# Attention and two mixture-of-experts layers: VectorE's operands in PSUM, routing in eleven steps, and the second matmul of the first layer's tiles as three fp32r products

## The chip, the cores and the metric

One Trainium2 chip, one of its cores. The metric is the device time of one execution in microseconds (us); the time of a kernel is the median of its runs. TensorE is named PE here, VectorE DVE, ScalarE ACT, GpSimd POOL and SyncE SP, as the profile does.

## The reference, cut to what matters

```python
# attention: B=2, H=8, S=768, D=64, 16 clusters
q_assign = argmax(q_n @ c_n.T); k_assign = argmax(k_n @ c_n.T)     # per head
scores = where(q_assign[:, None] == k_assign[None, :], scale * q @ k.T, -1e9)
attn = exp(scores - max(scores)); attn /= attn.sum(-1) + 1e-9
x = attn @ v                                                       # to [1536, 512]
# first MoE: N=1536, D=512, E=8 experts, F=1024
do = x @ w_skip > 0; e = argmax(x @ w_gate); g = softmax(x @ w_gate)[e]
x = x + where(do, g * (relu(x @ w1[e]) @ w2[e]), 0)
# second MoE: the same, no skip, at most 384 tokens of an expert, no residual
out = g2 * (relu(x @ w1b[e2]) @ w2b[e2])
```

All tensors are float32. Expert choices hang on an argmax, so float32 accuracy is wanted nearly everywhere: a product either runs in native fp32, or both factors are split into a high part of type fp32r and a rest, and three fp32r products (high·high, high·rest, rest·high) are added up.

## The kernel before, in words

The program has three stages in one launch: attention, the first MoE layer, the second one.

**Attention** works on 16 heads (two batches of eight) in pairs; a pair is a *group* g, 0 to 7. A head has six key chunks of 128, and a head's chunk is a *unit* u = 6·head + chunk, so a group has 12 units and there are 96. In a unit PE makes the scores of one key chunk against all 768 queries (`score_mm`, L293, four matmuls of 128x384), ACT takes the exponential (L301, tile P) and casts it to fp32r (L302, tile Ph), POOL makes the rest Pl = P − Ph (L304), and three units later PE adds the chunk to the outputs in six matmuls (`pv`, L319, L321, L323). Ahead of a head, `mpass` (L273) makes the scores once more with queries on the partitions, and DVE takes the row maximum of each (L274, tile m; the two halves of the queries' keys are joined by L277). `mrow` turns these maxima into a row (psR, L281), which DVE subtracts into BB (L282); the head's scores can't begin before that.

A group is prepared during the group before it. For g from 2 on: `prep_T` transposes queries and keys on PE into a PSUM tile psT (L147) and ACT copies it to SBUF (qkT, L149); `prep_H` casts it to fp32r on DVE (qkH, L157) and `prep_L` makes the rest there (qkL, L163); both read and write SBUF alone. `prep_as` multiplies with the centroids (psA, L190), `prep_oh` finds each token's cluster on DVE (L220 to L224, scratch tile `ad` in SBUF), `prep_mk` makes the mask rows from it (psM, L239), and `prep_V` casts the values (VA, L173, DVE) and takes their rest (VL, L174, POOL). Groups 0 and 1 have a preparation of their own. A finished group is divided by its row sums (`fin_den`, `fin_nat`: xn, L362) and its gate logits are added up (lgt, L371, and lg, L378 to L380).

**The order** of PE, ACT, POOL and SP is the written one: a table `at(u, function)` says in which unit each piece stands, and `hooks` does the same for pieces of the MoE layer. DVE's order is made by the framework's scheduler. An engine runs its instructions strictly in order. All PSUM scratch of attention comes from one pool `ps_w` of six banks (tag "w"), taken in turn; the outputs have two more banks.

**Routing of batch 0** happens while batch 1 is still in attention: `early1` to `early4`, at units 58, 60, 63 and 65, choose two experts A and B and their tokens with some 60 small DVE instructions, nearly all from SBUF to SBUF; gathers follow at unit 67 and the two experts' weights from unit 68 and 84.

**The first MoE** (`run`) has 11 tiles of 128 tokens, t = 0 to 10: the two of batch 0's experts, eight routed ones (t = 2 to 9) and one for the rest. A tile is 8 steps of the first matmul (`l1_steps`, L973, 32 matmuls of 128x128, weights as they are, native fp32), a ReLU on ACT, and 8 steps of the second matmul (`l2n_steps`, L1028, one native fp32 matmul of 128x512 for each 128 of the 1024 hidden values). Table `at(t, step)` places the rest in between: e0 to e3 find the second layer's gate for the finished tile (ro and rg, L1096, are two matmuls among them), and the weights of tile t+2 are loaded at steps 8 and 16 of tile t.

**The second MoE** splits its weights (`split`: ACT casts wh, L950, DVE subtracts wl, L951) and its hidden values (hl, L1311), and makes its second matmul in three fp32r products (`l2`, L1022 to L1024).

Of the kernel before, what the change touches and what calls it, by code (L numbers as in the profile page):

```python
# [9 lines left out]
F32 = mybir.dt.float32  # L10
# [12 lines left out]
def attention(ctx, tc, q, k, v, centroids, wcat, lgacc, xa, xb, idw, hooks, bind):  # L23
# [82 lines left out]
    st = {}  # L106
# [21 lines left out]
    def prep_T(g, i):  # L128
# [20 lines left out]
        nc.scalar.copy(s["T"][:, sl], ps)  # L149
# [53 lines left out]
    def prep_oh(g, parts=((0, 2),)):  # L203
# [3 lines left out]
        d = sm.tile([128, C, 2, 2, NC], F32, name="ad", bufs=1)  # L207
# [4 lines left out]
        for a, b in parts:  # L212
# [8 lines left out]
            nc.vector.tensor_tensor(out=f(d), in0=l, in1=m.to_broadcast(G), op=ALU.subtract)  # L221
            nc.vector.scalar_tensor_tensor(out=f(d), in0=f(d), scalar=0.0, in1=f(w), op0=ALU.is_ge, op1=ALU.mult)
            nc.vector.tensor_reduce(out=m, in_=f(d), axis=AX.X, op=ALU.max)
            nc.vector.tensor_tensor(out=f(o)[..., 0:NC], in0=f(d), in1=m.to_broadcast(G), op=ALU.is_equal)  # L224
# [42 lines left out]
    def mpass(h, qc):  # L267
# [70 lines left out]
    def fin_w(g):  # L338
        nc.vector.tensor_copy(idw[:, 128:], wcat[:, g % HP].rearrange("p h n -> p (h n)"))
# [12 lines left out]
    def fin_nat(g, i):  # L352
# [15 lines left out]
        if i == 0:  # L368
            s["lgt"] = sm.tile([128, C, 2, W], F32, name="lgt")
        t = s["lgt"]  # L370
        nc.vector.tensor_tensor(out=t[:, cs], in0=ps[:, :, 128:N].rearrange("p c (h n) -> p c h n", h=2),  # L371
                                in1=r.to_broadcast([128, n, 2, W]), op=ALU.mult)
        if i == 0:
            return
        for hh in range(2):
            acc = lgacc[:, b]
            if j == 0 and hh == 0:
                nc.vector.tensor_copy(acc, t[:, :, hh, :])  # L378
            else:
                nc.vector.tensor_tensor(out=acc, in0=acc, in1=t[:, :, hh, :], op=ALU.add)  # L380
        del st[g]
# [34 lines left out]
    for g in range(NP):  # L416
# [13 lines left out]
        else:  # L430
            w = (-10, -7, -7) if g == 1 else [u + x for x in (-23, -23, -21)]
            for i in range(3):
                at(w[i], prep_T, g, i)
            w = [(-6, -5, -3), (-6, -5, -4)] if g == 1 else [[u + x for x in (-17, -17, -14)], [u + x for x in (-21, -18, -16)]]
            for i in range(3):
                at(w[1][i], prep_H, g, i)
                at(w[0][i], prep_L, g, i)
# [29 lines left out]
class Moe:  # L467
# [242 lines left out]
    def early2(self):  # L710
        self.pre0 = self.prefix(self.oh0, self.T0, self.C)
        self.cnt0 = self.ps()[:, 0:self.E]
        self.nc.tensor.matmul(self.cnt0, self.ones, self.T0[:, 0], start=True, stop=True)

    def early3(self):
        V, sm, E, C = self.nc.vector, self.at, self.E, self.C
# [3 lines left out]
        V.scalar_tensor_tensor(out=key, in0=self.cnt0, scalar=16.0, in1=self.w8[:, 0, :], op0=ALU.mult, op1=ALU.add)  # L720
        esA = self.pick(key, ab[:, 0], "pA", sm)
        V.scalar_tensor_tensor(out=key, in0=ab[:, 0], scalar=-65536.0, in1=key, op0=ALU.mult, op1=ALU.add)
        esB = self.pick(key, ab[:, 1], "pB", sm)
        self.eA = self.expert(esA, "dA", sm)
        self.eB = self.expert(esB, "dB", sm)
        self.relabel(esA, esB, sm)
        self.rank(self.oh0, self.pre0, C, "a", sm, r0)
        t = sm.tile([128, 2, C, E], F32, name="abt")
        ia = sm.tile([128, 2, C], F32, name="inAB")
        kp = sm.tile([128, C], F32, name="kp0")  # L730
        for i in range(2):
            V.tensor_tensor(out=t[:, i], in0=self.oh0, in1=ab[:, i].unsqueeze(1).to_broadcast([128, C, E]), op=ALU.mult)
        V.tensor_reduce(out=ia, in_=t, axis=AX.X, op=ALU.add)
        for i in range(2):
            V.scalar_tensor_tensor(out=ia[:, i], in0=r0, scalar=128.0, in1=ia[:, i], op0=ALU.is_lt, op1=ALU.mult)
        V.tensor_tensor(out=kp, in0=ia[:, 0], in1=ia[:, 1], op=ALU.add)
        V.tensor_scalar(out=kp, in0=kp, scalar1=-1.0, scalar2=1.0, op0=ALU.mult, op1=ALU.add)
        V.tensor_tensor(out=kp, in0=kp, in1=self.sel[:, 0:C], op=ALU.mult)
        V.tensor_tensor(out=self.oh0, in0=self.bc(self.mx0, E), in1=self.order.unsqueeze(1).to_broadcast([128, C, E]), op=ALU.is_equal)
        V.tensor_tensor(out=self.ohp[1][:, 0:C], in0=self.oh0, in1=self.bc(kp, E), op=ALU.mult)  # L740
        self.R0 = self.at.tile([128, C, 128], BF16, name="R0")
        self.make_R(self.R0, r0, 0, C)
        self.rhs0 = self.at.tile([128, C, 2, 2], BF16, name="rhs0")
# [488 lines left out]
    def run(self, lg, cap):  # L1232
# [111 lines left out]
        for t in range(n1):  # L1344
# [14 lines left out]
            if t:  # L1359
# [5 lines left out]
                if t > 1:  # L1365
                    at(t, 16, loads(t + 2, 4, 8))
# [176 lines left out]
```

## Time and profile before

| | us |
|---|---|
| runs (three) | 708.2, 708.95, 710.4; median 708.95 |
| profiled execution, its own time | 708.59 |
| its span in the trace | 706.6 |
| PE busy | 655.8 (93%) |
| DVE busy | 416.7 (59%) |
| ACT busy | 344.9 (49%) |
| POOL busy | 267.2 (38%) |

The profile is one execution. "Busy" is the time in which an engine had an instruction under way; PE's clock is listed apart, as the share of full speed that was granted. A releaser ("<-DVE m") is the instruction that ended a wait. Stages lie in the trace roughly so: attention from 5 to 320, first MoE to 484, second MoE to the end.

### The profile page before, as it was taken

To read this page: it belongs to the slowest core of one execution; us is meant where nothing else is said; L and a number is where in the kernel's file an instruction comes from. 1 tells how busy PE (TensorE), PEld (TensorE's weight loads), DVE (VectorE), ACT (ScalarE), POOL (GpSimd) and SP (SyncE) were. 2 spreads that over 40 slices of the span, in tenths; PEclk is the share of its full clock that TensorE was granted. 3 is DMA by queue.
4 is the path that set the end of the run, shared out by engine and by line. 5 is a ranking of instruction groups with operands and counts; after the bars stand their busy time and mean duration, and the time that the engine had idled before them with its cause. 6 is when DMAs were issued, how large, how long until landed. Compare 5 with 4: busy or idle time off the path is not lost. (4 is left out here: it accounts for less than half of the span.)

```text
span 706.6 us, 11607 instructions
## 1 busy us (share of the span) xinstructions
PE 655.8 (93%) x4174; PEld 550.9 (78%) x4174; DVE 416.7 (59%) x964; ACT 344.9 (49%) x580; POOL 267.2 (38%) x194
## 2 busy tenths in 40 slices
PE   7879999898988989999999999997899999999993
PEld 6858979797966868888777777776688899889983
DVE  6888787878799887515524322225556764656430
ACT  4757877686865668871111111113236464646330
POOL 6665767576765657830211111100313023202210
PEclk9889999999999999999999999999999999999997
DMA  7953837383834659042177778772295666476100
GB/s 222 220 108 83 201 77 192 71 198 67 202 68 90 192 126 319 29 133 61 56 262 264 288 292 308 297 284 77 58 393 211 238 253 215 146 263 246 34 31 4
DMA packets 78966, 121.55 MB, mean 172 GB/s; under 512 B 27569, under 2 KB 42929, under 8 KB 78896
## 3 DMA queue, kind: packets, MB, share of 16 engines
q1 hardware_dynamic: 74416, 108.18, 50.1%
q0 software_dynamic: 4480, 12.50, 5.4%
q8 instruction: 37, 0.61, 0.4%
q14 instruction: 33, 0.27, 0.1%
HBM read 87.90 MB, written 13.37 MB: 143 GB/s over the span
## 5 line engine op out<-in xcount | busy, mean ns | idle before, releaser
L304 POOL TENSOR_TENSOR Pl<-P,Ph 128x768 fp32r<-128x768 f32 x93 | 173.2, 1868 | 88.2 <-ACT Ph L302 60.1
L274 DVE TENSOR_REDUCE m<-psx 128x1 f32<-128x384 f32 x192 | 97.1, 548 | 30.2 <-PE psx L273 29.6
L301 ACT ACTIVATE P<-pss 128x384 f32<-128x384 f32 x192 | 84.7, 490 | 58.5 <-PE pss L293 56.0
L293 PE MATMUL pss<-BB,AA 128*128 128x384 f32 (+1 forms) x384 | 91.2, 362 | 11.9 <-DVE m L274 11.9
L951 DVE TENSOR_TENSOR wl<-l,wh 128x1024 fp32r<-128x1024 f32 x60 | 70.3, 1221 | 30.5 <-ACT wh L950 30.5
L302 ACT CAST Ph<-P 128x768 fp32r<-128x768 f32 x96 | 80.1, 834 | 7.0 <-PE pso L321 4.1
L973 PE MATMUL psl<-xt,l 128*128 128x128 f32 x640 | 79.1, 280 | 3.7 <-PEq L1155 3.7
L973 PEld LDWEIGHTS psl<-xt,l 128*128 128x128 f32 x640 | 76.2, 195 | 8.2 <-issue 8.2
L293 PEld LDWEIGHTS pss<-BB,AA 128*128 128x128 f32 (+1 forms) x384 | 68.2, 197 | 18.2 <-DVE m L274 15.8
L1028 PE MATMUL psl<-l,hn 128*128 128x512 f32 x160 | 74.4, 602 | 0.0
L319 PE MATMUL pso<-Ph,VA 128*65 128x384 f32 x192 | 67.5, 351 | 0.4 <-ACT DN L336 0.4
L321 PE MATMUL pso<-Ph,VL 128*64 128x384 f32 x192 | 67.8, 353 | 0.0
L323 PE MATMUL pso<-Pl,VA 128*65 128x384 f32 x192 | 66.9, 348 | 0.1
L1053 POOL DMA_INDIRECT out_dram<-y,fsi x15 | 15.5, 1035 | 132.8 <-ACT y L1052 126.0
L1306 PE MATMUL psl<-xh,wh 128*128 128x256 f32 x224 | 62.9, 281 | 2.2 <-DVE hl L1311 2.2
L1307 PE MATMUL psl<-xl,wh 128*128 128x256 f32 x224 | 62.4, 279 | 0.7 <-DVE xl L1296 0.7
L1308 PE MATMUL psl<-xh,wl 128*128 128x256 f32 x224 | 62.3, 278 | 0.0
L950 ACT CAST wh<-l 128x1024 fp32r<-128x1024 f32 x60 | 59.0, 1046 | 0.5 <-DVE acco L1097 0.5
L273 PE MATMUL psx<-AA,BB 128*128 128x384 f32 x192 | 51.9, 365 | 7.0 <-DVE m L274 5.9
L1045 POOL DMA_INDIRECT xb<-x,fsi x8 | 8.1, 1014 | 111.7 <-DVE Rt L1060 111.7
L1022 PE MATMUL psl<-wh,hh 128*128 128x512 f32 x120 | 48.3, 403 | 0.0
L1028 PEld LDWEIGHTS psl<-l,hn 128*128 128x128 f32 x160 | 27.5, 191 | 25.7 <-issue 25.4
(384 smaller groups left out, 1187.0 us busy)
## 6 DMA issues: line engine op xcount, KB each, us to landing
l<-in_moe_w_dram SPq DMA_DIRECT2D x136, 512.0 KB, 6.1
AA<-qkH SPq DMA_DIRECT2D x14, 384.0 KB, 3.9
vn<-in_v_dram SPq DMA_DIRECT2D x8, 384.0 KB, 5.8
BB<-qkL SPq DMA_DIRECT2D x16, 192.0 KB, 3.1
xa<-xn SPq DMA_DIRECT2D x8, 384.0 KB, 3.1
xb<-xn SPq DMA_DIRECT2D x8, 384.0 KB, 4.2
AA<-qkL SPq DMA_DIRECT2D x31, 96.0 KB, 3.4
BB<-qkH SPq DMA_DIRECT2D x31, 96.0 KB, 3.0
```

The lines of the kernel that those rows point to most:

```text
L274: nc.vector.tensor_reduce(out=hs[h]["m2"][:, qc, f:f + 1], in_=ps, axis=AX.X, op=ALU.max)
L293: nc.tensor.matmul(ps, AA[0:K, t, kc * 128:(kc + 1) * 128], BB[0:K, t, sl], start=(t == 0), stop=(t == 1))
L301: nc.scalar.activation(out=P[:, f * HF:(f + 1) * HF], in_=ps, func=AF.Exp, scale=1.0 / 8.0)
L302: nc.scalar.copy(Ph, P)
L304: eng.tensor_tensor(out=Pl, in0=P, in1=Ph.bitcast(F32), op=ALU.subtract)
L319: nc.tensor.matmul(o[0:D + 1, :], va, Ph[:, sl], start=(kc == 0), stop=False)
L321: nc.tensor.matmul(o[0:D, :], vl, Ph[:, sl], start=False, stop=False)
L323: nc.tensor.matmul(o[0:D + 1, :], va, Pl[:, sl], start=False, stop=(kc == C - 1))
L951: nc.vector.tensor_tensor(out=l, in0=src, in1=h.bitcast(F32), op=ALU.subtract)
L973: nc.tensor.matmul(st[k][:, q, :], L1[c][:, f * 128:(f + 1) * 128], xt[:, c, :], start=(c == 0), stop=(c == 3))
L1028: self.nc.tensor.matmul(ps, h[:, f, 0:128], L2[f // 2][:, f % 2, :], start=(f == 0), stop=(f == 7))
L1306: nc.tensor.matmul(ps[:, q, :], wh[:, fs], xh[:, c, :], start=(c == 0), stop=False)
```

## The change

In attention, for groups from 2 on, `prep_T` now makes three tiles from the PSUM tile at once: ACT casts qkH from it (the cast stands where the copy stood), DVE copies qkT from it, and DVE makes qkL = psT − qkH with psT as an operand. `prep_H` and `prep_L` remain for group 1 alone, and `prep_T` stands two to three units later. ACT casts VA for every group. The tile `ad` is gone: `prep_oh` works in place in the PSUM tile psA. The maxima of the two halves are joined by a reduction with one input. The logits are scaled in place in PSUM. Routing of batch 0 is written anew as a generator `early` of eleven steps, at units 58 to 73, each with a PSUM bank for its scratch values, so that an instruction has at most one operand in SBUF; gathers and expert A's loads stand eight units later, expert B's where they were.

In the first MoE, tiles 2 to 9 make the second matmul with `l2`: three fp32r products in place of one native fp32 matmul. For that, the next tile's four chunks of w2 are split during tile t at steps 2, 5, 9 and 12 (of tile 1 at 8, 10, 12, 14), the ReLU writes a high part h1 (ACT) and a rest h1l (DVE), and w2 of tile t+3 is loaded at step 16 of tile t, where that of t+2 was.

```diff
 def prep_T(g, i):
-        nc.scalar.copy(s["T"][:, sl], ps)
+        nc.scalar.copy(s["H"][:, sl], ps)
+        nc.vector.tensor_copy(s["T"][:, sl], ps)
+        nc.vector.tensor_tensor(out=s["L"][:, sl], in0=ps, in1=s["H"].bitcast(F32)[:, sl], op=ALU.subtract)
 def prep_V(g):
-        if g < 2:
-            nc.scalar.copy(VA[:, :, :, 0:D], src)
-        else:
-            nc.vector.tensor_copy(VA[:, :, :, 0:D], src)
+        nc.scalar.copy(VA[:, :, :, 0:D], src)
 def prep_oh(g):
-            nc.vector.tensor_tensor(out=f(d), in0=l, in1=m.to_broadcast(G), op=ALU.subtract)
+            nc.vector.tensor_tensor(out=l, in0=l, in1=m.to_broadcast(G), op=ALU.subtract)
...
 def mpass(h, c):
-            m2 = hs[h]["m2"]
-            nc.vector.tensor_tensor(out=hs[h]["m"], in0=m2[:, :, 0], in1=m2[:, :, 1], op=ALU.max)
+            nc.vector.tensor_reduce(out=hs[h]["m"], in_=hs[h]["m2"], axis=AX.X, op=ALU.max)
 def fin_w(g):
-        nc.vector.tensor_copy(idw[:, 128:], wcat[:, g % HP].rearrange("p h n -> p (h n)"))
+        nc.scalar.copy(idw[:, 128:], wcat[:, g % HP].rearrange("p h n -> p (h n)"))
 def fin_nat(g, i):
-        nc.vector.tensor_tensor(out=t[:, cs], in0=ps[:, :, 128:N].rearrange("p c (h n) -> p c h n", h=2),
-                                in1=r.to_broadcast([128, n, 2, W]), op=ALU.mult)
+        t = ps[:, :, 128:N].rearrange("p c (h n) -> p c h n", h=2)
+        nc.vector.tensor_tensor(out=t, in0=t, in1=r.to_broadcast([128, n, 2, W]), op=ALU.mult)
...
-            w = (-10, -7, -7) if g == 1 else [u + x for x in (-23, -23, -21)]
+            w = (-10, -7, -7) if g == 1 else [u + x for x in (-21, -20, -18)]
```

```diff
-    def early1(self, lg):
+    def early(self, lg):
...
+        mxp, dp, val = scratch(C, C * E, C * E)
+        dp, val = by(dp, E), by(val, E)
+        V.tensor_reduce(out=mxp, in_=l0[:, :, 0:E], axis=AX.X, op=ALU.max)
+        V.tensor_tensor(out=dp, in0=l0[:, :, 0:E], in1=self.bc(mxp, E), op=ALU.subtract)
+        V.tensor_copy(d, dp)
+        V.scalar_tensor_tensor(out=val, in0=dp, scalar=0.0, in1=self.w8[:, 0:C, :], op0=ALU.is_ge, op1=ALU.mult)
...
+        yield
...
+    def l2_steps(self, hh, hl, W2):
...
+            self.l2(hh, hl, W2(), range(f, f + 1), st[0])
...
 def run(...):
-                if t > 1:
-                    at(t, 16, loads(t + 2, 4, 8))
+                if t < n1 - 1:
+                    for i, x in enumerate((8, 10, 12, 14) if t == 1 else (2, 5, 9, 12)):
+                        at(t, x, lambda t=t, i=i: split(t + 1, 4 + i))
+                    at(t, 16, loads(t + 3, 4, 8))
...
+            if 1 < t < n1:
+                steps = steps + self.l2_steps(*hh, lambda t=t: [SP[t, i] for i in range(4, 8)])
...
+        er = moe.early(lg)
+        for i in (0, 1, 2, 4, 6, 8, 9, 11, 12, 13, 15):
+            hooks.setdefault(u0 + i, []).append(lambda: next(er))
```

How instructions stand, at three places. DVE in attention, where group 3 is prepared while group 1 is finished, before:

```order
L362 TENSOR_TENSOR xn<-psN,rden 128x384
L371 TENSOR_TENSOR lgt<-psN,rden 128x102
L339 COPY idw<-wcat 128x34
...
L157 CAST qkH<-qkT 128x512 x2
L163 TENSOR_TENSOR qkL<-qkT,qkH 128x512
L274 TENSOR_REDUCE m_1119<-psx 128x1 x2
L163 TENSOR_TENSOR qkL<-qkT,qkH 128x512
L157 CAST qkH<-qkT 128x512
L274 TENSOR_REDUCE m_1119<-psx 128x1 x4
L163 TENSOR_TENSOR qkL<-qkT,qkH 128x512
L277 TENSOR_TENSOR m<-m_1119 128x6
```

and with the change:

```order
L359 TENSOR_TENSOR xn<-psN,rden 128x384
L366 TENSOR_TENSOR psN<-psN,rden 128x3x34
L370 COPY lg<-psN 128x51
L372 TENSOR_TENSOR lg<-psN,lg 128x51
L150 COPY qkT<-psT 128x512
L151 TENSOR_TENSOR qkL<-psT,qkH 128x512
L272 TENSOR_REDUCE m_1104<-psx 128x1 x2
L150 COPY qkT<-psT 128x512
L151 TENSOR_TENSOR qkL<-psT,qkH 128x512
L359 TENSOR_TENSOR xn<-psN,rden 128x384
...
L274 TENSOR_REDUCE m<-m_1104 128x6
```

The three pairs of cast and subtraction became three pairs of copy and subtraction, with PSUM among their operands, and the row maxima (m) stand around them as before. ACT over the same stretch, with the change:

```order
L332 COPY OT<-pso_1321 64x384
L333 COPY DN<-pso_1321 1x384
L172 CAST VA_173<-vn 128x12x64
L298 ACTIVATE P<-pss 128x384 x2
L299 CAST Ph<-P 128x768
L149 CAST qkH<-psT 128x512
L298 ACTIVATE P<-pss 128x384 x2
L299 CAST Ph<-P 128x768
L149 CAST qkH<-psT 128x512
L298 ACTIVATE P<-pss 128x384 x2
```

The cast VA stands behind the copies of a finished head (OT, DN), and each cast qkH behind a unit's exponentials. DVE in one routed tile of the first MoE, with the change (x, Rt and Mj finish the tile before; tg to g3T are the second layer's gate, on which rg rests):

```order
L1088 SCALAR_TENSOR_TENSOR x_5173<-psl_5097,fgs,xg 128x512
...
L981 TENSOR_TENSOR wl<-l_0_4983,wh 128x1024
L1054 SCALAR_TENSOR_TENSOR h1l<-psl_5180,h_5178 128x512
L981 TENSOR_TENSOR wl<-l_1_4985,wh 128x1024
...
L1128 TENSOR_TENSOR ro<-Mj,ohT 128x96
L1054 SCALAR_TENSOR_TENSOR h1l<-psl_5214,h_5178 128x512
L981 TENSOR_TENSOR wl<-l_2_4987,wh 128x1024
L1141 TENSOR_TENSOR acco<-acco,psq 128x96
...
L1135 TENSOR_TENSOR rg<-Mj,g3T 128x36
L981 TENSOR_TENSOR wl<-l_3_4989,wh 128x1024
```

The wl and h1l rows are new there; the others stood there before in the same order.

## Rows read from the trace of the kernel before

**Rows 1.** Page, the head: span and instructions.

```profile
span 706.6 us, 11607 instructions
```

**Rows 2.** Waits of PE from 20 to 286 us: total, times, longest.

```profile
PE pss L293 <- DVE m L274: 11.9, 8, 3.4
PE psx L273 <- DVE m L274: 5.9, 4, 4.6
PE psR L281 <- DVE m L277: 3.7, 2, 2.3
PE psM L239 <- DVE oh L224: 2.8, 6, 0.5
```

**Rows 3.** Windows: PE, PEld, DVE, ACT, POOL busy, PE clock, DMA share, GB/s.

```profile
20.00:34.00 14.00, 12.26 (x65) 11.41 (x64) 12.09 (x24) 9.31 (x17) 8.46 (x7) 0.76 1.01 224
34.00:286.00 252.00, 228.57 (x1385) 197.61 (x1384) 206.88 (x400) 179.64 (x327) 165.40 (x91) 0.95 0.58 143
```

**Rows 4.** Groups of DVE, 70 to 320 us: busy, mean ns, idle before.

```profile
L274 DVE TENSOR_REDUCE m<-psx 128x1 f32<-128x384 f32 x149 | 75.7, 549 | 26.4 <-PE psx L273 25.9
L163 DVE TENSOR_TENSOR qkL<-qkT,qkH 128x512 fp32r<-128x512 f32 x15 | 20.3, 1375 | 0.0
L157 DVE CAST qkH<-qkT 128x512 fp32r<-128x512 f32 x15 | 13.3, 912 | 0.0
L173 DVE CAST VA<-vn 128x768 fp32r<-128x768 f32 x6 | 11.5, 1909 | 0.0
L277 DVE TENSOR_TENSOR m<-m 128x6 f32<-128x6 f32 x13 | 5.8, 450 | 0.1
```

**Rows 5.** Single lines, whole run: shortest/median/longest ns, first and last start us.

```profile
L157 DVE CAST qkH<-qkT x21: 410/421/3889, 7.5 to 244.3; 128x512 fp32r<-128x512 f32 x21
L163 DVE TENSOR_TENSOR qkL<-qkT,qkH x21: 676/693/2340, 7.9 to 249.8; 128x512 fp32r<-128x512 f32 x21
L277 DVE TENSOR_TENSOR m<-m x16: 152/154/1756, 24.4 to 291.1; 128x6 f32<-128x6 f32 x16
L362 DVE TENSOR_TENSOR xn<-psN,rden x16: 556/558/559, 79.9 to 319.2; 128x384 f32<-128x384 f32 x16
L142 DVE COPY qkT<-psT x2: 683/684/685, 16.9 to 19.8; 64x512 f32<-64x512 f32 x2
L171 ACT CAST VA<-vn x2: 830/836/842, 17.4 to 24.5; 128x768 fp32r<-128x768 f32 x2
L654 DVE COPY einf<-psq x1: 153/153/153, 234.7 to 234.7; 128x4 f32<-128x4 f32 x1
```

**Rows 6.** Timeline of DVE, 31 to 52 us: start, us, instruction.

```profile
41.02 4.04 DVE L157 CAST qkH<-qkT 128x512 fp32r<-128x512 f32 x2
44.98 4.52 DVE L163 TENSOR_TENSOR qkL<-qkT,qkH 128x512 fp32r<-128x512 f32 x2
```

**Rows 7.** Timeline of PE, 45 to 70 us.

```profile
50.02 1.47 PE L273 MATMUL psx<-AA,BB 128*128 128x384 f32 x3 [4.62 <-DVE m L274]
```

**Rows 8.** Timeline of PE, 395 to 430 us, a tile's second matmul.

```profile
403.96 1.88 PE L1028 MATMUL psl<-l,hn 128*128 128x512 f32 x4
405.68 0.21 PE L1096 MATMUL psq<-ro,Rt 128*128 128x96 bf16 x1
```

**Rows 9.** Timeline of PE, 528.8 to 534.5 us, a second matmul in three products.

```profile
528.88 0.40 PE L1022 MATMUL psl<-wh,hh 128*128 128x512 f32 x1
534.40 0.27 PE L961 MATMUL psxT<-idw,xg 128*128 128x128 f32 x1
```

**Rows 10.** Window of one routed tile, columns as in rows 3.

```profile
404.00:420.00 16.00, 16.00 (x101) 11.95 (x100) 3.80 (x19) 2.46 (x5) 2.03 (x2) 1.00 0.77 287
```

**Rows 11.** Single lines of the second MoE, columns as in rows 5.

```profile
L951 DVE TENSOR_TENSOR wl<-l,wh x60: 1215/1220/1228, 490.6 to 687.0; 128x1024 fp32r<-128x1024 f32 x60
L950 ACT CAST wh<-l x60: 1034/1046/1066, 482.0 to 685.5; 128x1024 fp32r<-128x1024 f32 x60
L1311 DVE SCALAR_TENSOR_TENSOR hl<-psl,hh x28: 684/691/693, 521.3 to 672.2; 128x512 fp32r<-128x512 f32 x28
```

More of the change, by code (lines that the diff above doesn't have):

```diff
@@ L379, in fin_nat @@
             else:
-                nc.vector.tensor_tensor(out=acc, in0=acc, in1=t[:, :, hh, :], op=ALU.add)
-        del st[g]
+                nc.vector.tensor_tensor(out=acc, in0=t[:, :, hh, :], in1=acc, op=ALU.add)
+        if i:
+            del st[g]
     sched = {}
@@ L430, in attention @@
         else:
-            w = (-10, -7, -7) if g == 1 else [u + x for x in (-23, -23, -21)]
+            w = (-10, -7, -7) if g == 1 else [u + x for x in (-21, -20, -18)]
             for i in range(3):
                 at(w[i], prep_T, g, i)
[L434 to L437, printed above, removed]
+            if g == 1:
+                for i, (l, h) in enumerate(zip((-6, -5, -3), (-6, -5, -4))):
+                    at(h, prep_H, g, i)
+                    at(l, prep_L, g, i)
             w = (-5, -4, -3) if g == 1 else [u + x for x in (-19, -17, -16)]
@@ L710, in early2 @@
[L710 to L716, printed above, removed]
-        r0 = sm.tile([128, C], F32, name="r0")
-        key = sm.tile([128, E], F32, name="key")
-        ab = sm.tile([128, 2, E], F32, name="ab")
[L720 to L730, printed above, removed]
-        for i in range(2):
[L732 to L743, printed above, removed]
-        self.rhs05 = self.at.tile([128, C, 2, 5], BF16, name="rhs05")
-        for i in range(2):
-            V.tensor_tensor(out=self.rhs0[:, :, i], in0=self.cols2[:, 0:C], in1=self.bc(ia[:, i], 2), op=ALU.mult)
-            V.tensor_tensor(out=self.rhs05[:, :, i], in0=self.cols5[:, 0:C], in1=self.bc(ia[:, i], 5), op=ALU.mult)
@@ L761, in relabel @@
         V.tensor_copy(self.namei, x)
-    def early4(self):
-        p1 = self.spread(self.R0, self.rhs0, self.C)
-        p2 = self.spread(self.R0, self.rhs05, self.C)
-        inf, t, S = self.ids(p1, 2, self.rt, "e")
+        V.tensor_copy(xs, x)
+        yield
+        ia = sm.tile([128, 2, C], F32, name="inAB")
+        ta = sm.tile([128, 2, C, E], F32, name="abt")
+        ks = sm.tile([128, C], F32, name="kp0")
+        abp, iap, kp = scratch(2 * E, 2 * C, C)
+        abp, iap = by(abp, E), by(iap, C)
@@ new lines, in early @@
+        V.tensor_copy(abp, ab)
+        for i in range(2):
+            V.tensor_tensor(out=ta[:, i], in0=abp[:, i].unsqueeze(1).to_broadcast([128, C, E]), in1=oh0, op=ALU.mult)
+        V.tensor_reduce(out=iap, in_=ta, axis=AX.X, op=ALU.add)
+        for i in range(2):
+            V.scalar_tensor_tensor(out=iap[:, i], in0=r0, scalar=128.0, in1=iap[:, i], op0=ALU.is_lt, op1=ALU.mult)
+        V.tensor_reduce(out=kp, in_=iap.rearrange("p i c -> p c i"), axis=AX.X, op=ALU.add)
+        V.tensor_scalar(out=kp, in0=kp, scalar1=-1.0, scalar2=1.0, op0=ALU.mult, op1=ALU.add)
@@ new lines, in early @@
+        V.tensor_tensor(out=ks, in0=kp, in1=self.sel[:, 0:C], op=ALU.mult)
+        V.tensor_copy(ia, iap)
+        yield
+        rhs0 = sm.tile([128, C, 2, 2], BF16, name="rhs0")
+        rhs05 = sm.tile([128, C, 2, 5], BF16, name="rhs05")
+        mxp, o, iap = scratch(C, C * E, 2 * C)
+        o, iap = by(o, E), by(iap, C)
+        V.tensor_copy(mxp, mx)
+        V.tensor_copy(iap, ia)
+        V.tensor_tensor(out=o, in0=self.bc(mxp, E), in1=self.order.unsqueeze(1).to_broadcast([128, C, E]), op=ALU.is_equal)
@@ new lines, in early @@
+        V.tensor_tensor(out=self.ohp[1][:, 0:C], in0=o, in1=self.bc(ks, E), op=ALU.mult)
+        for i in range(2):
+            V.tensor_tensor(out=rhs0[:, :, i], in0=self.bc(iap[:, i], 2), in1=self.cols2[:, 0:C], op=ALU.mult)
+            V.tensor_tensor(out=rhs05[:, :, i], in0=self.bc(iap[:, i], 5), in1=self.cols5[:, 0:C], op=ALU.mult)
+        yield
+        R0 = sm.tile([128, C, 128], BF16, name="R0")
+        for i in (0, 3):
+            self.make_R(R0, r0, i, i + 3)
+            yield
@@ L767, in early4 @@
+        inf, t, S = self.ids(self.spread(R0, rhs0, C), 2, self.rt, "e")
+        self.rest(self.spread(R0, rhs05, C), 2, S, self.rt, "e")
         self.dests(inf, t, 2, S, self.rt, "e")
-        self.rest(p2, 2, S, self.rt, "e")
         self.S1 = S
+        yield
     def route1(self, lg):
@@ L977, in l1_steps, with step @@
         return [lambda f=f: step(f) for f in range(8)]
+    def l2_steps(self, hh, hl, W2):
+        st = {}
+        def step(f):
+            if f == 0:
+                st[0] = self.ps2()
+            self.l2(hh, hl, W2(), range(f, f + 1), st[0])
+            return st[0]
+        return [lambda f=f: step(f) for f in range(8)]
     def l2n_steps(self, h, L2):
@@ L1033, in new_h, with new_h1 @@
         return hh, hl
+    def new_h1(self):
+        return [self.big.tile([128, 8, 128], F32R, tag=x, name=x) for x in ("h1", "h1l")]
     def new_hn(self, n):
```

123 lines of the change are left out of this document (77 added, 46 removed).

## The prediction, written before the run

> **What bounds the kernel now.** I read the page first: the span [rows 1] and the busy shares (the table above). PE's high share would say "PE-bound", but it is an average, so I went stage by stage with three views: PE's waits, windows of busy time with the granted clock, and DVE's groups by line.
>
> In attention the waits of PE between 20 and 286 us come from one place [rows 2]: DVE's row maxima m and, more rarely, the tile oh. The four rows add up to 11.9 + 5.9 + 3.7 + 2.8 = 24.3 us. No row there names ACT, POOL or a DMA. The windows say the same from another side [rows 3]: PE is busy 12.26 of 14 us and 228.57 of 252 us, so it stands still for 1.74 + 23.43 = 25.2 us. They also show a second loss: the mean granted clock is 0.76 and 0.95 of full speed. Where a stretch W ran at clock c, at most (1 − c)·W can be got back: 3.4 and 12.6 us. A wait and the clock go together: the longest wait, 4.62 us, ends at 50.02 [rows 7], and the stretch around it is one of those below full clock. So attention has 25.2 + 16.0 = about 41 us in which PE was waiting or slowed, of which 36.0 lie after 34 us.
>
> Why is m late? Its reduction is not slow: 549 ns on the average of 149 [rows 4]. What stands before it in DVE's order is. The cast qkH takes 421 ns at the median but 912 on the average after 70 us; qkL 693 and 1375; the tiny joining of two halves, 154 and 450 [rows 4, 5]. Their longest are 3889, 2340 and 1756 ns. An instruction of six elements that takes 1.76 us once isn't computing, it is held up. The excess over the median is 15 × 0.491 = 7.4 us for qkH, 15 × 0.682 = 10.2 for qkL and 13 × 0.296 = 3.8 for the joining. These lines read and write SBUF only. xn, with an operand in PSUM and one in SBUF, took between 556 and 559 ns in all 16 cases, and the copies from PSUM 683 to 685 [rows 5]. One place shows it whole: at 41.02 us two qkH took 4.04 us and two qkL 4.52 [rows 6], where the medians give 0.84 and 1.39. PE's 4.62 us of waiting ends right after [rows 7].
>
> In the first MoE there is nothing to wait for: in a routed tile PE is busy 16.00 of 16 us at full clock, DVE 3.80 and ACT 2.46 [rows 10]. That stage is bound by PE's own work.
>
> **The change part by part.**
> *qkT, qkH, qkL.* ACT does one cast where it did one copy: no more work. DVE copies T at 0.684 us and subtracts at 0.691, the price of hl, which has the same operands in the same places and size [rows 5, 11]. For the 15 of each in rows 4, DVE spent 20.3 + 13.3 = 33.6 us and will spend 15 × 1.375 = 20.6. Both prices hardly vary in their rows.
> *VA.* DVE loses 11.5 us; ACT gets 6 × 0.836 = 5.0 [rows 4, 5]. ACT was busy 179.64 of 252 us [rows 3], so this lies beside PE's work.
> *The joining of m*: 5.8 us become 13 × 0.154 = 2.0.
> *oh, logits, idw, the routing's small instructions*: the same arithmetic, more copies, fewer held up. A single small instruction costs the same either way (a 4-element copy from PSUM took 153 ns, the shortest joining in SBUF 152 [rows 5]). I cost this part at nothing: its held-up instructions and the additional copies roughly cancel. Its cover is DVE's slack; without it some 25 copies of 0.16 us, 4 us, would show.
> So DVE sheds 13.0 + 11.5 + 3.8 = 28 us of its 207, above all where m waits in line.
> What of the 41 us comes back? Lower end: nothing, if another wait takes over at once. Upper end: all of it. The 5.1 us before 34 us belong to groups 0 and 1, whose preparation hardly changes; I leave them. Of the other 36.0 I take five sixths, **30 us**: it is nearest to the upper end since all the waiting in rows 2 hangs on one engine, and the sixth is left for first halves of chains that DVE still has to compute (oh before the mask, BB before the scores).
>
> *Second matmul of eight tiles.* Native: two hidden blocks from 403.96 to 405.68, so 0.86 us each [rows 8]. In three products: eight blocks from 528.88 to 534.40, so 0.69 each [rows 9]. Saved: 8 tiles × 8 × 0.17 = 10.9 us. Added per tile: on DVE four wl of 1.220 and two h1l of 0.691, 6.3 us, to 3.80 + 6.3 = 10.1 of 14.6 us; on ACT four casts of 1.046, to 6.6 [rows 10, 11]. Both lie beside PE, but DVE's order puts the gate (rg) behind three wl, and rg is due two thirds through the second matmul. I take off 0.9 for that: **10 us**. The w2 loads move a tile ahead on SP's queue, behind slots that the split has freed by then; at 287 GB/s and a DMA share of 0.77 [rows 10] a tile of 14.6 us would need 0.84, so they stay hidden.
>
> The sum is 708.59 − 30 − 10 = **668.6 us**, made against the profiled execution, which lies 0.4 us below the median of the runs shown.
>
> [...] A copy of a few elements from PSUM took 153 ns where one instruction of that size in SBUF took 152 [rows 5]: no surcharge. [...]
>
> **The rivals.**
> *B: PSUM banks run short.* A psT bank was free after ACT's copy; now it is held through a cast, a copy of 0.684 and a subtraction of 0.691, 1.4 us longer, 18 times; psA is held through three more passes, some 1.6 us, 6 times; each routing step holds one too. All from six banks in turn. Against: no row of rows 2 waits for a bank. For: the margin isn't shown. Between nothing and 18 × 1.4 + 6 × 1.6 = 35 us; a third of it, 12, leaves attention 18 us, and with its gates later the MoE 9: 708.6 − 27 = 681.6 us.
> *C: the MoE tiles gain little.* If the splits hold DVE so that rg or the ReLU's rest comes late by 0.9 us in each of eight tiles, 7 of the 10 us go: 708.6 − 30 − 3 = 675.6 us.
> *D: the hold-ups stay*, that is, the change doesn't do what it says. Then the MoE's 10 us are all: 698.6 us. Against it stand the rows of xn and of the copies from PSUM, which never vary while POOL works beside them [rows 5]. [...]
> *E: slower.* The subtraction now waits in DVE's order for ACT's cast, and all later m stand behind it. ACT works 179.64 / 84 = 2.1 us per unit (252 us hold 84 units of 3 us) [rows 3]. DVE's slack after the change is 252 − 207 + 28 = 73 us, so 18 waits of over 73 / 18 = 4.1 us each would make DVE the bound. With two units' work and VA ahead of the cast, 4.2 + 0.8 = 5.0 us, attention grows by 18 × 0.9 = 17 us: 708.6 + 17 − 10 = 715.4 us. Against: the cast stands right behind one unit's exponentials, so 2 to 3 us are likelier; it decides only past 4.1.
>
> **How the numbers follow.** A has 62 in 100, B 20, C 10, D 4, E 3; one is left for a mishap that I can't name. The likeliest gives 668.6. Its own range is 659 (36 and 11 back, plus a little of the clock before 34 us) to 678 (attention two thirds of 30). For 8 in 10 over all cases the upper end must take in B with some 6 us more of its 35 lost: 659 to 687. A measurement of this kernel can tell some 0.3%, 2 us, from no change. A, B, C and D all lie further below than that: faster 0.96; the same 0.01; slower 0.03, from E.
>
> **What would show it.** Right: the copies and subtractions of rows 4's two lines at a steady 0.68 to 0.69 us, no small instruction of 1.8 us in routing, PE's waits on m below 8 us between 20 us and the end of attention, the clock there at 0.98 or more; second matmuls at 0.69 us a block and tiles every 14.6 us. Wrong: PE waiting for ACT's cast or for a bank's last reader (B, E), m waiting behind qkL while qkL waits for ACT (E), waits at the rg matmul (C), or DVE rows that still vary (D). If attention's end moves by 30 us and the total doesn't, loads of the first MoE's weights were the next thing late.

## The result, and the profile after

The changed kernel took 680.12 us (median of four runs, 677.97 to 681.07), the kernel before on the same chip 708.86; the ratio is 0.9587 with a 95% interval of 0.956 to 0.9615. Faster, then, and inside the range of 659 to 687, but 11.5 us above the 668.6 that I gave. The profiled execution took 680.39 us, its span is 678.7. So the two traces compared here lie 28.2 us apart, where the forecast had summed up 40.

Three marks on PE cut the program into pieces: attention's last output matmul, the last native second matmul of the first MoE (tile 10), and the end. The rows are for single lines: shortest, median and longest duration in ns, then the first and the last start. Kernel before:

```profile
L293 PE MATMUL pss<-BB,AA x384: 331/340/686, 28.0 to 308.4; 128*128 128x384 f32 x192
L323 PE MATMUL pso<-Pl,VA x192: 331/337/562, 36.5 to 312.9; 128*65 128x384 f32 x192
L1028 PE MATMUL psl<-l,hn x160: 592/593/677, 337.7 to 497.6; 128*128 128x512 f32 x160
```

Changed kernel:

```profile
L290 PE MATMUL pss<-BB,AA x384: 331/338/522, 26.7 to 286.7; 128*128 128x384 f32 x192
L320 PE MATMUL pso<-Pl,VA x192: 331/338/387, 33.8 to 291.4; 128*65 128x384 f32 x192
L1069 PE MATMUL psl<-l,hn x32: 592/592/676, 316.2 to 468.4; 128*128 128x512 f32 x32
```

Attention ends 312.9 − 291.4 = 21.5 us earlier; the stretch from there to the last native second matmul shrank from 184.7 to 177.0, 7.7 us; the rest of the program took 209.0 and then 210.3, 1.3 us more. 21.5 + 7.7 − 1.3 = 27.9, the difference of the spans. The 1.3 us are PE's busy time, 192.6 and then 193.8 us for the same 1305 instructions, at a granted clock of 0.98 and then 0.97; PE's idle time there is 16.5 us in both traces. Why the clock was granted less is not shown. I call the time from the first score to the last output matmul "attention's length": 284.9 us before, 264.7 now.

The views that carried the prediction, of the changed kernel. PE's waits from 20 to 286 us (against [rows 2]):

```profile
PE pss L290 <- DVE lg L372: 3.6, 4, 1.2
PE pss L290 <- ACT P L298: 2.1, 3, 1.0
PE psx L271 <- DVE m L272: 1.4, 3, 0.5
PE pss L290 <- DVE key L744: 1.2, 1, 1.2
PE psR L278 <- DVE m L274: 1.0, 1, 1.0
PE pss L290 <- DVE ab L748: 0.9, 1, 0.9
PE psx L271 <- ACT P L298: 0.9, 2, 0.7
PE pso L316 <- ACT DN L333: 0.7, 3, 0.2
PE pss L290 <- DVE m L272: 0.6, 2, 0.5
```

Windows, columns as in [rows 3]:

```profile
20.00:34.00 14.00, 12.05 (x67) 10.64 (x66) 13.21 (x27) 10.43 (x18) 9.63 (x7) 0.88 0.98 222
34.00:286.00 252.00, 240.46 (x1507) 206.07 (x1506) 170.59 (x425) 202.60 (x373) 178.59 (x99) 1.00 0.61 152
```

DVE's lines that stand where those of [rows 5] stood:

```profile
L150 DVE COPY qkT<-psT x18: 679/683/693, 39.5 to 218.3; 128x512 f32<-128x512 f32 x18
L151 DVE TENSOR_TENSOR qkL<-psT,qkH x18: 680/681/684, 40.1 to 219.0; 128x512 fp32r<-128x512 f32 x18
L274 DVE TENSOR_REDUCE m<-m x16: 166/166/170, 24.5 to 269.4; 128x6 f32<-128x12 f32 x16
```

What to read there: the durations became constant, as forecast. The granted clock after 34 us rose from 0.95 to 1.00. And PE's idle time fell only from 25.2 us to 1.95 + 11.54 = 13.5. The waits of pss and psx for m fell from 11.9 + 5.9 us to 0.6 + 1.4, but the scores (pss) now wait for other instructions than before: lg and ab, which are DVE's last readers of psN and of a routing bank, key, and ACT's P. (key reads no bank last. It ends at 210.08 us, an lg on psN at 210.01, and PE goes on at 210.16, 0.15 us after that lg as in the case below; so this wait, too, is one for psN's bank.)

Those windows hold different amounts of work. Over attention's length, which holds the same 1561 PE instructions in both traces, the first two columns and PE's clock are comparable (kernel before, then changed kernel):

```profile
28.00:312.90 284.90, 260.61 (x1561) 224.56 (x1561) 222.63 (x429) 207.09 (x377) 186.62 (x102) 0.95 0.57 139
26.70:291.40 264.70, 251.97 (x1561) 215.27 (x1561) 180.17 (x442) 212.19 (x391) 185.12 (x103) 0.99 0.61 151
```

So of the 20.2 us by which the length shrank, 24.3 − 12.7 = 11.6 are PE's idle time and 8.6 its busy time, in which the higher clock has a part that these rows don't part from the rest. The other 1.3 of the 21.5 us lie before the first score.

One of these new waits at close range. DVE, then PE, of the changed kernel; start, us, instruction:

```profile
107.13 0.56 DVE L359 TENSOR_TENSOR xn<-psN,rden 128x384 f32<-128x384 f32 x1 [0.45 <-PE psN L357]
107.79 0.27 DVE L366 TENSOR_TENSOR psN<-psN,rden 128x102 f32<-128x102 f32 x1
108.09 0.46 DVE L372 TENSOR_TENSOR lg<-psN,lg 128x51 f32<-128x51 f32 x2
```

```profile
106.93 0.60 PE L290 MATMUL pss<-BB,AA 128*128 128x384 f32 x2
108.70 0.59 PE L290 MATMUL pss<-BB,AA 128*128 128x384 f32 x2 [1.17 <-DVE lg L372]
```

A score matmul reads BB and AA and writes a scratch bank; it has no business with lg except that lg is the last to read the bank. PE goes on 0.15 us after it.

The two longest of [rows 2] have to be read in the same way. A matmul of psx or pss doesn't read m either; the reduction m (L274) is the last reader of a psx bank. DVE, then PE, of the kernel before:

```profile
122.52 4.57 DVE L163 TENSOR_TENSOR qkL<-qkT,qkH 128x512 fp32r<-128x512 f32 x2
127.01 1.94 DVE L274 TENSOR_REDUCE m<-psx 128x1 f32<-128x384 f32 x4
```

```profile
122.64 0.89 PE L273 MATMUL psx<-AA,BB 128*128 128x384 f32 x4
123.55 0.30 PE L190 MATMUL psA<-cblk,qkT 128*128 128x32 f32 x2
...
125.10 0.52 PE L293 MATMUL pss<-BB,AA 128*128 128x384 f32 x2
127.61 2.29 PE L293 MATMUL pss<-BB,AA 128*128 128x384 f32 x6 [1.99 <-DVE m L274]
```

Four tiles psx, one psA and one pss (two matmuls each) take the six banks in turn; the next score wants the first psx's bank, and starts when the first of the four reductions, late behind two held-up qkL, has read it. So 11.9 + 5.9 = 17.8 of the 24.3 us of [rows 2] were waits for a bank: the kernel before was short of banks already whenever DVE was late.

In the first MoE, a tile's second matmul (PE's timeline, first two hidden blocks, and the next tile's first):

```profile
365.90 0.48 PE L1063 MATMUL psl<-wh,h 128*128 128x512 f32 x1
366.22 0.40 PE L1064 MATMUL psl<-wh,h1l 128*128 128x512 f32 x1
...
367.38 0.22 PE L1140 MATMUL psq<-ro,Rt 128*128 128x96 bf16 x1
367.42 0.48 PE L1063 MATMUL psl<-wh,h 128*128 128x512 f32 x1
...
380.77 0.48 PE L1063 MATMUL psl<-wh,h 128*128 128x512 f32 x1
```

The period is 380.77 − 365.90 = 14.87 us where it was 16.00. A product starts every 0.23 us, but the first one behind another kind of matmul takes 0.32.

### The profile page after: what moved, and what is told of

It is laid out like the page before. It is cut to its first block, busy times and chain, and to the rows that moved or that the text cites. A ratio compares the mean times of both kernels' runs of the same rounds, so it can differ in the third digit from the quotient of the medians.

```text
span 678.7 us, 11860 instructions
## 1 busy us (share of the span) xinstructions
PE 638.1 (94%) x4238; PEld 552.5 (81%) x4238; DVE 418.5 (62%) x1024; ACT 380.3 (56%) x626; POOL 265.7 (39%) x194
## 5 line engine op out<-in xcount | busy, mean ns | idle before, releaser
L301 POOL TENSOR_TENSOR Pl<-P,Ph 128x768 fp32r<-128x768 f32 x93 | 170.5, 1843 | 67.4 <-ACT Ph L299 32.8
L981 DVE TENSOR_TENSOR wl<-l,wh 128x1024 fp32r<-128x1024 f32 x92 | 109.4, 1221 | 51.1 <-ACT wh L980 50.6
L290 PE MATMUL pss<-BB,AA 128*128 128x384 f32 (+1 forms) x384 | 88.8, 354 | 8.7 <-DVE lg L372 3.6
L980 ACT CAST wh<-l 128x1024 fp32r<-128x1024 f32 x92 | 92.3, 1046 | 0.5 <-DVE acco L1141 0.5
L1003 PE MATMUL psl<-xt,l 128*128 128x128 f32 x640 | 80.9, 283 | 4.6 <-PEq L1199 4.6
L290 PEld LDWEIGHTS pss<-BB,AA 128*128 128x128 f32 (+1 forms) x384 | 66.6, 192 | 14.6 <-PE pss L290 3.3
L316 PE MATMUL pso<-Ph,VA 128*65 128x384 f32 x192 | 65.6, 342 | 0.7 <-ACT DN L333 0.7
L318 PE MATMUL pso<-Ph,VL 128*64 128x384 f32 x192 | 65.7, 342 | 0.0
L1065 PE MATMUL psl<-wl,hh 128*128 128x512 f32 x120 | 47.1, 393 | 0.0
L1064 PE MATMUL psl<-wh,hl 128*128 128x512 f32 x120 | 46.9, 391 | 0.0
```

Of the source, the lines that this page charges most:

```text
L290: nc.tensor.matmul(ps, AA[0:K, t, kc * 128:(kc + 1) * 128], BB[0:K, t, sl], start=(t == 0), stop=(t == 1))
L301: eng.tensor_tensor(out=Pl, in0=P, in1=Ph.bitcast(F32), op=ALU.subtract)
L316: nc.tensor.matmul(o[0:D + 1, :], va, Ph[:, sl], start=(kc == 0), stop=False)
L318: nc.tensor.matmul(o[0:D, :], vl, Ph[:, sl], start=False, stop=False)
L980: nc.scalar.copy(h, src)
L981: nc.vector.tensor_tensor(out=l, in0=src, in1=h.bitcast(F32), op=ALU.subtract)
```

## The experiments

Times are compared by their ratio to runs of the kernel before on the same chip, with 95% intervals; the changed kernel's is 0.9587. Lengths come from one trace each; three pairs of kernels with the same attention code differ by 2.3, 1.3 and 0.2 us, so a length tells apart some 3 us and no less.

### The two parts alone

The first has the hunks of attention and routing, the second those of the first MoE.

> The change's attention and routing, with the first MoE as before. If the two parts add up: attention's last output matmul comes 21.5 us earlier, as in the changed kernel, and the time is 708.9 - 21.5 = 687 us (686 to 689). Rival: the parts help or hurt one another (loads of the MoE's weights, or DVE's late work), then it is off that by over 3 us.

> The three products in the first MoE's eight tiles, with attention and routing as before. If the parts add up: 708.9 - 7.7 = 701 us (700 to 703), a tile every 14.87 us. Rival (the splits crowd DVE only because attention ends earlier): the waits for x in tiles 1 and 2 are gone and it is 699.5 or less.

Attention alone: ratio 0.967 (0.961 to 0.9729), at 708.9 us some 685.5, a little under the 686 to 689 expected; attention's last output matmul comes 19.9 us earlier, length 267.0 us, the MoE stretch 184.6. The MoE alone: 0.989 (0.9806 to 0.9974), length 285.1, the stretch 177.7. The parts add up within the intervals: 3.3% + 1.1% against 4.1%. The rival on the waits for x in the MoE falls: the trace of the MoE alone has the same two waits of 1.6 us in sum, with attention ending as late as ever.

### Which part of attention

First the preparation as before:

```diff
-        nc.scalar.copy(s["H"][:, sl], ps)
-        nc.vector.tensor_copy(s["T"][:, sl], ps)
-        nc.vector.tensor_tensor(out=s["L"][:, sl], in0=ps, in1=s["H"].bitcast(F32)[:, sl], op=ALU.subtract)
+        nc.scalar.copy(s["T"][:, sl], ps)
...
+            nc.vector.tensor_copy(VA[:, :, :, 0:D], src)
```

> The changed kernel with the preparation of the groups as before (qkT copied by ACT, qkH and qkL by DVE from SBUF, VA by DVE). Theory (these long instructions with SBUF operands are held up and stand ahead of m): PE's waits on m of some 2 us a group return, qkH and qkL again take up to 2 to 4 us, 692 to 698 us. Rival (the small instructions were what mattered): 682 to 684 us.

Ratio 0.9736 (0.9668 to 0.9804), length 273.3 us. PE's waits in its trace:

```profile
PE pss L291 <- DVE m L273: 11.5, 7, 2.5
PE psx L272 <- DVE m L273: 3.3, 2, 3.0
```

The waits on m are back, and 8.6 of the 20.2 us by which attention's length had shrunk are gone. In the same run qkL's mean after 70 us is 1419 ns again. The theory's mechanism holds; its number, 692 to 698 us, was a little high (0.9736 × 708.9 = 690.2). Then the routing in four steps as before:

```diff
+        for _k, _v in ((3, [early]), (u0, [lambda: moe.early1(lg)]), (u0 + 2, [moe.early2]), (u0 + 5, [moe.early3]), (u0 + 7, [moe.early4]), (u0 + 9, [moe.startA, moe.gatherAB]), (u1 + -14, [moe.xtA]), (u1 - 18, [swap]), (u1 + 2, [lambda: moe.l1A(0)]), (u1 + 6, [lambda: moe.l1A(1)])):
```

> The changed kernel with routing of batch 0 as before (four steps, scratch in SBUF). Theory (hold-ups of the small instructions): waits of 1 to 3.4 us on m between units 58 and 70 return, 684 to 687 us. Rival (each of the eleven steps costs a bank and gives back what it frees): within 1 us of the changed kernel, 679 to 681 us.

Ratio 0.9596 (0.9534 to 0.9657): the times don't tell it from the changed kernel. In the trace three small instructions took 1.67, 1.77 and 1.78 us again (names and order, eight elements each), and PE waited once, for 5.1 us (psL on m); on the other side the waits on key and ab are gone. The length is 268.0 us, 3.3 above the changed kernel's. The rival comes out better: that the eleven steps give back about what they free fits both. The routing was a large part of the edit, and no part of the time that this run can tell.

### What held DVE up

In the kernel before, POOL's subtraction is replaced by a memset of the same tile:

```diff
-        eng.tensor_tensor(out=Pl, in0=P, in1=Ph.bitcast(F32), op=ALU.subtract)
+        if eng is nc.vector:
+            eng.tensor_tensor(out=Pl, in0=P, in1=Ph.bitcast(F32), op=ALU.subtract)
+        else:
+            eng.memset(Pl.bitcast(F32), 0.0)
```

> The kernel before, with the rest Pl on POOL replaced by a memset to zero of the same tile: this leaves out the low part of the exponentials, and POOL's instructions then write SBUF and read nothing. Theory (an instruction of DVE with two SBUF inputs is held up by what POOL reads there): qkL takes 0.69 us every time and the joining of m 0.15, while qkH, a one-input cast, may still be held up by what POOL writes. Rival (DVE is held up by something else, the DMAs or ACT): qkL still reaches 1.4 us or more, as before.

One execution, the profiled one: 670.45 us. DVE's lines, whole run, to be held against [rows 5]:

```profile
L157 DVE CAST qkH<-qkT x21: 410/420/1056, 7.4 to 210.7; 128x512 fp32r<-128x512 f32 x21
L163 DVE TENSOR_TENSOR qkL<-qkT,qkH x21: 673/680/693, 7.9 to 211.4; 128x512 fp32r<-128x512 f32 x21
L173 DVE CAST VA<-vn x6: 548/550/552, 65.8 to 224.4; 128x768 fp32r<-128x768 f32 x6
L277 DVE TENSOR_TENSOR m<-m x16: 146/158/422, 24.2 to 253.1; 128x6 f32<-128x6 f32 x16
```

For qkL the cause is settled: its longest fell from 2340 to 693 ns, and nothing of DVE was touched. Six of the 21 ran while POOL had a memset of Pl under way, and these took 675 to 692 ns; so it is POOL's reading, not POOL's being at work, and not the DMAs or ACT. Two instructions with two SBUF inputs were still held up, each beside a subtraction that POOL keeps in this run: one joining of m (422 ns, beside a qkL of POOL's) and names in the routing (1737 ns, beside VL). So the joining's 0.15 came in 15 of 16 cases. qkH is held up beside a memset too: five of the 21 took 754 to 1056 ns, each with a memset under way, which reads nothing. VA fell from 1909 [rows 4] to 550 ns, but no memset ran during any of the six, so this run doesn't show whether writing alone would hold it up.

The run gives the size too. Attention in it:

```profile
L293 PE MATMUL pss<-BB,AA x384: 331/338/522, 27.6 to 270.1; 128*128 128x384 f32 x192
L326 PE MATMUL pso<-Pl,VA x192: 331/336/386, 35.5 to 274.6; 128*65 128x384 f32 x192
```

Its last matmul starts 312.9 − 274.6 = 38.3 us earlier than before, the length is 247.0. My upper end of 41 us was no fiction: a kernel nearly without the hold-ups gets most of it. In it PE's waits of pss and psx for m are 0.8 us in all, with the same six banks: where DVE isn't late, they suffice. (The memset takes 0.74 us where the subtraction took 1.84, so POOL is also done sooner; this much of the 38 can't be taken apart. In the changed kernel, next run, both together are worth 3.8 us of attention's length.) The changed kernel gets 21.5. Is the rest still POOL? The same memset in the changed kernel:

> The changed kernel with POOL's rest Pl as a memset to zero (this leaves out the low part of the exponentials), so POOL reads nothing for it. From first score to last output matmul, attention took 284.9 us before, 264.7 in the changed kernel, 247.0 in the kernel before with the same memset. Theory (the hold-ups are gone from the changed kernel, and what is left of the gap to 247 are banks held by DVE and ACT's extra work): attention stays at 260 to 265 us. Rival (POOL still holds up DVE or is itself late with Pl in the changed kernel): it falls to 250 us or less.

```profile
L290 PE MATMUL pss<-BB,AA x384: 331/338/452, 27.6 to 283.9; 128*128 128x384 f32 x192
L323 PE MATMUL pso<-Pl,VA x192: 331/337/387, 34.3 to 288.5; 128*65 128x384 f32 x192
```

Ratio 0.9524 (0.9502 to 0.9547), length 260.9 us. The theory's 260 to 265 came. Its waits on lg, key, ab and P (3.2, 1.2, 0.9 and 3.7 us) are about those of the changed kernel. So POOL no longer matters much there: with the same memset in both, attention is 13.9 us longer with the change than without it, and the change itself brought these in. By the windows of the two lengths 9.1 of them are PE's idle time (11.3 and 2.2 us) and 4.8 its busy time, at a granted clock of 1.00 and 0.99.

### Banks

Five scratch banks instead of six, in either kernel:

```diff
-    ps_w = ctx.enter_context(tc.tile_pool(name="ps_w", bufs=6, space=PSUM))
+    ps_w = ctx.enter_context(tc.tile_pool(name="ps_w", bufs=5, space=PSUM))
```

> The changed kernel with five scratch banks in attention instead of six. Theory (banks limit the changed kernel, since DVE holds them longer): at least 5 us slower than the changed kernel, more waits of the scores that end with DVE's last reader of a bank. Rival (banks don't matter): 679 to 682 us.

> The kernel before with five scratch banks in attention. Theory (its banks were free early, since ACT's copy alone held psT): slower by 0 to 4 us, clearly less than what the changed kernel loses by the same edit. Rival (both are as short of banks): it loses as much as the changed kernel, 5 us or more.

Changed kernel with five: ratio 0.9914 (0.9881 to 0.9946), length 284.2 us, which is 3.3% of 709, some 23 us, lost, all of attention's gain. Kernel before with five: 1.01 (1.006 to 1.0139), 7 us lost, length 290.2, which is over the 0 to 4 that I expected of it, and under a third of the other's loss. Waits of the changed kernel with five banks:

```profile
PE pss L290 <- DVE lg L372: 4.7, 4, 1.2
PE psx L271 <- DVE qkL L151: 4.0, 1, 4.0
PE psN L357 <- DVE BB L279: 2.8, 5, 0.6
PE psx L271 <- ACT P L298: 2.3, 11, 0.4
```

None of these four pairs is a matmul and its operand: each is a matmul and the last reader of the bank that it wants. In the kernel before with five banks every wait of PE over 0.5 us still names m or oh, and the waits of pss and psx for m, which are waits for a bank, grew from 17.8 to 20.3 us. A bank is worth three times as much to the changed kernel; that DVE reads more of them there, and for longer (psN in two instructions of 0.56 and 0.25 us before, in four of 0.55, 0.27, 0.21 and 0.21 with the change), fits this.

### Giving banks back

First the logits: DVE scales them from PSUM into an SBUF tile, one instruction, and POOL adds them up two units later.

```diff
+        nc.vector.tensor_tensor(out=s["lgt"][:, cs], in0=ps[:, :, 128:N].rearrange("p c (h n) -> p c h n", h=2),
+                                in1=r.to_broadcast([128, n, 2, W]), op=ALU.mult)
+
+    def fin_lg(g):
...
+                nc.gpsimd.tensor_tensor(out=acc, in0=acc, in1=t[:, :, hh, :], op=ALU.add)
```

> The changed kernel with the scaled logits written from PSUM to an SBUF tile and added up by POOL two units later, so that the bank of psN is free after two DVE instructions and not four. Theory (the four waits of 0.8 to 1.2 us that end with lg are waits for that bank): they shrink to 0.5 us or less each, 1.5 to 4 us faster than the changed kernel in the same ratio, 676 to 678.5 us at a time before of 708.9. Rival (the same scores wait for ACT or for m a moment later): the named releaser changes and the time stays within 1 us of 680.

Its waits of the scores of 1 us and more (the four that named lg have no successor):

```profile
PE pss L290 <- ACT P L298: 2.0, 3, 1.0
PE pss L290 <- DVE ab L754: 1.5, 1, 1.5
```

The length is 260.8 us, ratio 0.9558 (0.9523 to 0.9592). These waits are gone, as expected, and that on key with them; the time moved by the 2 us or so that this is worth, too little for the intervals to part. Then, on top of it, qkT copied from PSUM by ACT:

```diff
-        nc.vector.tensor_copy(s["T"][:, sl], ps)
+        nc.scalar.copy(s["T"][:, sl], ps)
```

> The changed kernel with logits added by POOL, and qkT copied from PSUM by ACT, so DVE makes only qkL of the three and the psT bank is held some 0.7 us less. Theory (banks held by DVE are the limit): attention 3 us or more under the 260.8 us of the kernel with POOL's logits alone. Rival (ACT, busy for 188 of 232 us there, is now as near to the limit): waits on ACT's P grow by 2 us or more and attention takes 261 to 266 us.

Length 264.6 us, ratio 0.9557 (0.9529 to 0.9585); waits on P are 3.9 us where they were 2.9. My theory missed. The rival's 261 to 266 us hold, though the growth of the waits, 1.0, is under its 2: relieving DVE and the bank at ACT's cost gains nothing. That ACT is the next limit fits this and isn't shown; of the 3.8 us by which the length grew, only 0.9 are PE's idle time (9.5 and 10.5), and the clock was 0.98 where it was 1.00.

### The late split

On top of POOL's logits, the fourth split of tiles 1 and 3 is written after the tile's end:

```diff
-                    for i, x in enumerate((8, 10, 12, 14) if t == 1 else (2, 5, 9, 12)):
-                        at(t, x, lambda t=t, i=i: split(t + 1, 4 + i))
+                    for i, x in enumerate((8, 10, 12, 17) if t == 1 else (2, 5, 9, 19) if t == 3 else (2, 5, 9, 12)):
+                        at(*divmod(17 * t + x, 17), lambda t=t, i=i: split(t + 1, 4 + i))
```

> The changed kernel with logits added by POOL, and in the first MoE the fourth split of tiles 1 and 3 behind the tile's last instruction x. Theory (the waits of 0.62 and 0.98 us for x come from the split that stands before it on DVE): both are gone, the MoE stage is 1.0 to 1.6 us shorter, total 2.5 to 5.5 us under the changed kernel at equal ratio, 675 to 677.5 us at a time before of 708.9. Rival (the four slots' loads or the next tile's second matmul then wait for the late split): no gain over the kernel with POOL's logits alone.

The place that it aims at, in the changed kernel; DVE, then PE:

```profile
356.82 1.21 DVE L981 TENSOR_TENSOR wl<-l,wh 128x1024 fp32r<-128x1024 f32 x1
357.95 0.18 DVE L1141 TENSOR_TENSOR accg<-accg,psq 128x36 f32<-128x36 f32 x1
358.05 0.74 DVE L1088 SCALAR_TENSOR_TENSOR x<-psl,fgs,xg 128x512 f32<-128x512 f32 x1
```

```profile
358.85 0.66 PE L991 MATMUL psxT<-idw,x 128*128 128x128 f32 x4 [0.98 <-DVE x L1088]
```

Both waits are gone and the MoE stretch fell from 177.5 to 174.7 us, more than the 1.6 of the waits, so that the first MoE gains 184.7 − 174.7 = 10.0 us over the kernel before. Ratio 0.9525 (0.9499 to 0.9552), 676.65 us on its chip: faster than the kernel before and, since the intervals lie apart, than the changed kernel, by 0.6% or 4.4 us for the two edits together; from POOL's logits alone (0.9523 to 0.9592) the interval doesn't part it. It is the version to keep.

Last, in that kernel VA by DVE again:

> The kernel of the run before (POOL's logits, late splits) with VA cast by DVE again, from SBUF to SBUF, for groups 2 to 7. Theory (a cast from SBUF is held up by POOL, and m waits behind it): VA takes 1.7 to 1.9 us again, waits on m grow by 3 us or more, attention takes 265 to 270 us where it took 260.8 and 262.1. Rival (ACT's load is the nearer limit in attention, and 5 us are taken off it): waits on ACT's P go and attention takes 257 to 260 us.

Ratio 0.9536 (0.9492 to 0.9581), length 263.7 us. VA took 1940 ns at the median again (706 once; 1909 on the average before, 550 with the memset), so it is held up as before; but with everything around it out of SBUF, m has slack for it (a single longer wait on m, 2.3 us), and ACT's relief shows no gain either. Neither set of numbers came; this part of the change can't be told from no change here.

## Why the prediction was right, and where its number failed

*The bound.* Right as to DVE. m was late because DVE's instructions with SBUF operands were held up (qkL up to 2340 ns), and the memset run shows by what (693 ns at most without POOL's subtraction), which the prediction had only inferred from one engine's rows. Wrong in one reading: it says that no row of [rows 2] waits for a bank, and the two largest do (17.8 of 24.3 us, above).

*Prices on DVE.* Right: copy 0.683, subtraction 0.681 against 0.684 and 0.691; the joining 0.166 against 0.154.

*"Of the other 36.0 I take five sixths, 30 us."* The mechanism is right and this is the term that was mis-sized: it measured 21.5. I had kept a sixth for "first halves of chains that DVE still has to compute"; the runs show instead that PE, which stood still for 23.4 us after 34 us, still does for 11.5, since the scores go on waiting for banks, now held by other readers: 4.8 us on psN (named lg and key), 0.9 on a routing bank (ab) and 3.0 on P of ACT. The term that I costed "at nothing", the logits and the routing, is where the first two sit: not by DVE's time, which I weighed, but by the bank that DVE holds meanwhile, which I weighed, in rival B, for psT, psA and the routing's steps and not for psN. The granted clock came back nearly whole (0.95 and then 1.00 after 34 us; in the kernel before it was 0.50 from 50.02 to 54.00 us, right behind the longest wait), but the busy time fell by 8.6 us, where the term rested on 12.6 for the clock after 34 us.

*Second matmul, 10 us.* Mis-sized by 2.3: 7.7. The period fell by 1.13 us, not 1.36 less 0.11, since the first product behind each inserted small matmul takes 0.32 us and not 0.23, which [rows 9], a stretch without insertions, couldn't show. rg was never late; x was, in two tiles (0.62 and 0.98), where DVE had the last split and other work in front. 8 × 1.13 less these 1.6 is 7.4 of the 7.7. DMA stayed hidden at a share of 0.84 and 315 GB/s in a tile's window, as worked out.

*The range.* The likeliest case's own, 659 to 678, doesn't hold the 680.12; the stated one does, because its upper end was drawn to take in rival B.

*The rivals.* B is what came in part: it priced bank shortage at 12 us and gave 681.6 us, and its mechanism is shown by the waits at close range and by the five-bank runs. That its number is 1.5 us off is partly luck: it has 18 us for attention and 9 for the MoE, and 21.5, 7.7 and −1.3 came. I gave it 20 in 100 because no row of before waits for a bank. That premise was false; [rows 2] showed a kernel without a bank to spare. C's place was wrong, its mechanism (a split ahead of something PE needs) came in small. D falls by the constant rows; of the small instructions one with two SBUF inputs, esi behind the routing's steps, still took 1.82 us. E's start was there, DVE waits 10.3 us in all for ACT's casts, 8 times, 1.3 us each, far from the 4.1 at which it would have decided. (Its sum is 708.6 + 17 − 10 = 715.6, not 715.4; nothing hangs on it.)

*Small instructions.* The prediction has them at the same cost in PSUM as in SBUF, from one row of each (153 and 152 ns). In the changed kernel a copy of eight elements out of PSUM, in the routing, takes

```profile
L756 DVE COPY names<-psq x2: 155/156/156, 216.9 to 219.6; 128x8 f32<-128x8 f32 x2
```

and one and the same instruction (order, eight elements) took 159 ns with its source in SBUF before and takes 167 with it in PSUM now, 8 ns more.

What stays open: the 13.9 us of attention's length between the two kernels with the memset (260.9 and 247.0). PE's idle time makes 9.1 of them, and the waits on banks and on ACT name most of that; the 4.8 us of busy time have no name. Open too is why the clock was granted less behind the first MoE.

## What to carry to other kernels

Moving an operand from SBUF to PSUM spared DVE the hold-ups beside POOL's reads here (qkL took 680 to 684 ns in 18 cases, where it had taken up to 2340), but it made a bank's life longer (psT was read by one copy of 0.59 us before, and by a cast of 0.59, a copy of 0.68 and a subtraction of 0.68 with the change): count, per bank, the instructions between its first write and its last read, before and after, next to the number of banks. Nearly all waits for a bank named its last reader here (m, 17.8 us before; lg, 3.6 us with the change), so check each wait in the trace of before: does the waiting matmul read what that instruction writes? If not, banks are short already. A cheap way to learn the margin is to take one bank away. And when a long chain of waits is removed, ask what stands behind it: here half of PE's idle time stayed (12.7 of 24.3 us).

## What the runs showed that I had not expected

One bank of six was worth 23 us to one kernel and 7 to the other, with the same matmuls in attention. A memset on POOL in place of a subtraction took 38 us off a kernel in which POOL was busy 38% of the time and PE waited for it once, 1.6 us at the start: here POOL held up a stage through what it read beside DVE, without being waited for. (A part of the 38 can be POOL's shorter time.) And in the changed kernel the same memset was worth under 1% (ratios 0.9524 and 0.9587).
